# A second output-projection tile cut to seven rows a partition, its rest fetched in 8 KB pieces through GpSimd's queue

## The chip, the cores and the metric

One core of one Trainium2 chip runs the whole program. The metric is the device time of one execution in microseconds. The kernel before takes 393.38 us, the median of three runs (393.32 to 393.49).

## The reference

The program is one decode step of a transformer block with adaptive layer norm, for eight sequences of one token each, all in float32. The part that matters here is attention over a window of 2,048 cached positions and the projection by `wo` behind it:

```python
W = min(4096, max(256, Sk // 4))                      # 2048 of 8192 positions
q = (x @ wq).reshape(B, Sq, Hq, Dh).transpose(0, 2, 1, 3)
k = repeat(k_cache[:, :, Sk - W:, :], rep, axis=1)    # 8 kv heads, 4 query heads each
v = repeat(v_cache[:, :, Sk - W:, :], rep, axis=1)
p = softmax(einsum("bhqd,bhkd->bhqk", q, k) * Dh**-0.5)
o = einsum("bhqk,bhkd->bhqd", p, v)
A = o.transpose(0, 2, 1, 3).reshape(B, Sq, Hq * Dh) @ wo    # wo: 4096 x 512
...
mod = (silu(c) @ w_mod).reshape(B, 6, 1, 512)         # sa, ca, ga, sb, cb, gb
h = layernorm(x) * (1 + ca) + sa
x = x + ga * A(h)
h = layernorm(x) * (1 + cb) + sb
x = x + gb * (relu(h @ w1 + b1) ** 2 @ w2 + b2)
```

## The kernel before

Everything that the program needs from HBM is read once, about 165 MB, nearly all of it K and V.

**Loads and their order.** A list `loads` fixes the order: the two parts of `w_mod`, `wq`, then K and V tiles of 4 MB (32 KB in each of 128 partitions), with the `wo` tiles put between them, and the MLP's weights last. `pump` walks the list and stops at the first entry for whose size no buffer is free: there are four big buffers of 4 MB (in the tile `home`) and one small buffer of 2 MB (the tile `small`). `done(key)` gives a buffer back and calls `pump` again. All these loads are issued by SyncE (SP in the profile), one after the other on one queue, and SP waits in that order for the buffers to come free. The small buffer carries in turn the second part of `w_mod`, the `wo` tiles 0, `far`, 1, 2 and half of `w1`.

**A loop over 38 steps `s`.** Two steps belong to one K tile: VectorE transposes it (`transposes`, L216), TensorE makes the scores (`scores`, L387). A softmax follows every fourth step. Five steps later the V tile is multiplied (`weighted`, L473), and after every fourth of those steps `gather` (L508) sorts one kv head's output into `oT`, in which entry `i` of eight stands for the rows `8p + i` of a `wo` tile.

**The output projection.** `project_o(j)` multiplies `oT` with `wo` tile `j` (1,024 rows, 2 MB) and adds up in `wo_ps`. It runs at `s` = 14, 22, 30 and after the loop. Tile 0 is already held in another form: each group of 32 rows gives its first 28 rows to four partitions, seven rows each, so that the tile has 14 KB in each of 128 partitions. The last four rows of each group (128 rows in all, 256 KB) are the entry `far`. `far` is loaded in three pieces by SP (L143, L144) into a few partitions of the small buffer, which GpSimd (POOL) has cleared before (L139). Four small matmuls (L537) with the selector `fsel` bring the matching rows of `oT` into `oX`, and `far_rows` (L549, at `s` = 18) adds these rows' share. `gather` uses another split of its columns for the kv heads of tile 0.

**What frees what.** `project_o(1)` frees the small buffer at `s` = 22, and the next entry of the list, `wo` tile 2, is issued then by SP, behind the V load that stands ahead of it.

Of the kernel before, what the change touches and what calls it, by code (L numbers as in the profile page):

```python
# [19 lines left out]
def tile_adaln_cached_attention_mlp(  # L20
# [52 lines left out]
    eps = consts.tile([P, 1], F32, name="eps")  # L73
    nc.vector.memset(eps, EPS)
    fsel = consts.tile([P, 4, P], F32, name="fsel")
    nc.gpsimd.memset(fsel, 0.0)
    for y in range(2):
        nc.gpsimd.tensor_copy(
            fsel[:, :, 32 * y : 32 * y + 12].rearrange("p r (q a) -> p r q a", a=4),
            ident.rearrange("p (y a r q) -> p y r q a", y=2, a=4, r=4)[:, y, :, :3],  # L80
        )
    nc.gpsimd.tensor_copy(
        fsel[:, :, H : H + 32].rearrange("p r (h x) -> p r h x", x=4)[..., 3],
        ident.rearrange("p (h r q) -> p r h q", r=4, q=4)[..., 3],
    )
    oX = consts.tile([P, 8, 32], F32, name="oX")

# [15 lines left out]
    def load(key):  # L103
        kind, i = key
        held[key] = free[size_of(key)].pop(0)
        if key == ("wq", 0):
            return
        t = slots[size_of(key)][held[key]]
        if kind in "KV":

            hk, c = divmod(i, 2)
            v = k_cache[4 * c : 4 * c + 4, hk] if kind == "K" else v_cache[c::2, hk]
            v = v[:, SK - W :, :].rearrange("u (p j) d -> p u (j d)", j=NJ)
            cuts = (0, big // 2, big) if key == ("V", 2 * HKV - 1) else (0, big)
            for x, y in zip(cuts, cuts[1:]):
                nc.sync.dma_start(t[:, x:y], v[..., x:y])
            return

        def rows(o, v):
            n = v.shape[1] * v.shape[2]  # L120
            nc.sync.dma_start(t[:, o : o + n].rearrange("p (a n) -> p a n", n=v.shape[2]), v)

        w1v = w1.rearrange("(p kc) n -> p kc n", p=P)

        def wo_rows(j):

            r = 2 * REP * DH
            if j == 0:
                v = wo[:r].rearrange("(b s) n -> b s n", s=32)[:, :28].rearrange("b (g i) n -> b g (i n)", i=7)
                nc.sync.dma_start(t[:, : 7 * D], v)  # L130
                return
            v = wo[j * r : (j + 1) * r, :].rearrange("(p i) n -> p (i n)", p=P)
            nc.sync.dma_start(t[:, : big // 2], v)

        if kind == "wo":
            wo_rows(i)
        elif kind == "far":

            nc.gpsimd.memset(t[:H], 0.0)  # L139
            v = wo[: 2 * REP * DH].rearrange("(h q s) n -> q h s n", q=4, s=32)[:, :, 28:]  # L140
            v = v.rearrange("q h r n -> q h (r n)")
            for y in range(2):
                nc.sync.dma_start(t[32 * y : 32 * y + 12, : 4 * D], v[:3, 4 * y : 4 * y + 4])  # L143
            nc.sync.dma_start(t[3:32:4, 4 * D :], v[3])  # L144
        elif kind == "mod":

            v = w_mod.rearrange("(p kc) n -> p (kc n)", p=P)
            nc.sync.dma_start(t, v[:, big:] if i else v[:, :big])
        elif kind == "wq":

            o = base[held["wq", 0]]
            nc.sync.dma_start(home[:, o : o + 2 * big], wq.rearrange("(p k) n -> p (k n)", p=P))
        elif kind == "tail":
            wo_rows(HKV // 2 - 1)
# [12 lines left out]

    loads = [("mod", 0), ("mod", 1), ("wq", 0), ("wq", 1), ("K", 0), ("K", 1)]
    for n in range(2, 2 * HKV):
        if n == 9:  # L170
            loads.append(("far", 0))
        if n in (4, 11, 13):
            loads.append(("wo", (4, 11, 13).index(n)))
        loads += [("K", n), ("V", n - 2)]
    loads += [("V", 2 * HKV - 2), ("V", 2 * HKV - 1), ("tail", 0), ("w1", 0), ("w2", 0)]
    at = [0]
# [6 lines left out]
    def done(*keys):  # L183
        for k in keys:
            free[size_of(k)].append(held.pop(k))
        pump()
# [306 lines left out]
    def gather(hk):  # L493

        o = OS_.pop(hk)
        b = slice(H * (hk % 2), H * (hk % 2) + H)
        pp = ps_m.tile([P, 512], F32, name="m_ps", tag="m_ps")
        for x in range(2):
            to = pp[b].rearrange("p (d x e i) -> p x e d i", x=2, e=2, i=8)[:, x]
            cuts = [(to, o.rearrange("p e (d i) -> p e d i", i=8))]  # L500
            if hk < 2:
                o = o.rearrange("p e (q s) -> p (e q) s", s=32)
                cuts = [
                    (to[..., :7], o[:, :, :28].rearrange("p a (g i) -> p a g i", i=7)),
                    (to[..., 7].rearrange("p e (r q) -> p e q r", r=4), o[:, :, 28:]),
                ]
# [12 lines left out]

    def project_o(j):  # L520

        last = j == HKV // 2 - 1
        key = ("tail", 0) if last else ("wo", j)
        w = slot(key, D)
        for i in range(8 if j else 7):
            nc.tensor.matmul(
                wo_ps[32 * (i % 4) : 32 * (i % 4) + 32, :],
                oT[:, i, :],
                w[:, i, :],
                start=(j == 0 and i < 4),  # L530
                stop=(last and i >= 4),
            )
        if j == 0:

            px = ps_m.tile([P, 512], F32, name="m_ps", tag="m_ps")
            for r in range(4):
                nc.tensor.matmul(px[:, 32 * r : 32 * r + 32], fsel[:, r], oT[:, 7, :], start=True, stop=True)  # L537
            px = px[:, :P].rearrange("p (r b) -> p r b", b=32)
            nc.scalar.copy(oX[:H, :4], px[:H])
            nc.scalar.copy(oX[:32, 4:], px[H : H + 32])  # L540
        if not last:
            done(key)

    def far_rows():

        w = slot(("far", 0), D)
        for r in range(8):
            k = H if r < 4 else 32
            nc.tensor.matmul(  # L549
                wo_ps[32 * (r % 4) : 32 * (r % 4) + 32, :], oX[:k, r], w[:k, r, :], start=False, stop=False  # L550
            )
        done(("far", 0))

    def late_tiles():

# [13 lines left out]
    for s in range(N + PV_LAG + 1):  # L569
        g, i = divmod(s, C)  # L570
        q, h = divmod(s, 2)
        v = s - PV_LAG
        soft = 1 <= g <= HKV
        ends = v >= C and v % C == 0
        if i == 1 and soft and g < HKV:
            soft_e(g - 1)
        if s < N:
            transposes(q, 2 * h, 0)
        if 1 <= s <= N:
            scores((s - 1) // 2, 2 * ((s - 1) % 2) + 1)  # L580
            if i == 0:
                soft_a(g - 1)
        if s < N:
            transposes(q, 2 * h, 1)
        if i == 1 and soft:
            soft_f(g - 1)
        if v > C and v % (2 * C) == 1 and v < N:
            project_o(v // C // 2 - 1)
        if s == 18:
            far_rows()  # L590
        if 1 <= v <= N:
            weighted(v - 1, 1)
        if i == 0 and soft:
            soft_b(g - 1)
        if s < N:
            transposes(q, 2 * h + 1, 0)
        if i == 1 and soft:
            soft_g(g - 1)
            if g == HKV:
                rT, b1_in, b2_in, x1, h2T = late_tiles()  # L600
        if i == 0 and soft:
            soft_c(g - 1)
        if 1 <= v <= N and v % 2 == 0:
            parts(v // 2 - 1)
# [132 lines left out]
```

## Time and profile before

| What | Value |
|---|---|
| Median of three runs | 393.38 us (393.32 to 393.49) |
| The profiled execution: its own time | 393.28 us |
| The profiled execution: span from first to last instruction | 391.5 us |
| TensorE (PE), share of the span | 66% |
| VectorE (DVE), share of the span | 57% |
| ScalarE (ACT), share of the span | 12% |
| GpSimd (POOL), share of the span | 2% |
| SP's DMA queue, share of 16 engines | 98.3% |
| Read from HBM | 164.67 MB, 421 GB/s over the span |

The core has 16 DMA engines, and a transfer into 128 partitions is split over all of them. The profile gives their mean busy share, in 40 slices of the span or in any stretch that one asks for, and a share under 1 near the end says that some of them have run out of work. The rows of a stretch have the busy time of each compute engine, then the granted clock, the DMA share and the GB/s. In the list of waits a row names who waited, for whom, and then the total in us, the number of waits and the longest one.

### The profile page before, as it was taken

The page shows a single profiled execution, that of the slowest core. Times are in us where ns is not written, and L with a number is a line of the kernel's source. Part 1 is how long each engine was busy: PE and PEld are TensorE (multiplying, and loading weights), DVE is VectorE, ACT ScalarE, POOL GpSimd, SP SyncE. Part 2 cuts the span into 40 slices and gives each one's busy share as a digit, 9 for nine tenths or more (in the row PEclk, how much of TensorE's full clock was granted, in tenths as well). Part 3 has the DMA queues.
Part 4 walks back from the last instruction along what each step waited for, and adds up shares of the span by engine and source line. Part 5 has one row for each costly group of instructions (what it writes and reads, how often), then busy time and mean ns, then how long its engine had stood idle before and what let it go on. Part 6 is the DMA issues. An engine that isn't in the chain of part 4 may idle for free.

```text
span 391.5 us, 4765 instructions
## 1 busy us (share of the span) xinstructions
PE 258.8 (66%) x2050; PEld 79.7 (20%) x2050; DVE 224.0 (57%) x314; ACT 46.7 (12%) x91; POOL 5.9 (2%) x13
## 2 busy tenths in 40 slices
PE   0080959868437873797379828783773737996896
PEld 0030210112112320232122202220221212222333
DVE  1370099878057835874577456490776357854322
ACT  0120111311003100310031003100200003004010
POOL 1000000000000000030000000000000000000000
PEclk9996889998859996999599968988796969997999
DMA  8999999999999999999999999999999999999994
GB/s 330 437 429 426 437 435 442 435 424 411 431 432 432 437 432 435 430 427 429 444 417 435 430 432 432 427 429 427 415 445 437 429 429 431 425 423 424 421 432 190
DMA packets 6915, 165.04 MB, mean 422 GB/s; under 512 B 806, under 2 KB 974, under 8 KB 1230
## 3 DMA queue, kind: packets, MB, share of 16 engines
q1 hardware_dynamic: 6814, 164.70, 98.3%
q8 instruction: 16, 0.26, 0.3%
q10 hardware_dynamic: 80, 0.04, 0.0%
q14 instruction: 5, 0.04, 0.0%
HBM read 164.67 MB, written 0.07 MB: 421 GB/s over the span
## 4 chain that ended last, share of the span: by engine, by line
DMA 59%; DVE 22%; PE 14%; issue 4%; SPq 0%; ACT 0%; DVEq 0%; ACTq 0%
DMA home<-in_A_k_cache_dram 37%; DVE kT L216 12%; DMA home<-in_A_wq_dram 9%; DMA home<-in_B_w_dram 7%; DMA home<-in_A_v_cache_dram 6%; PE s_ps L387 5%; DVE pT L453 4%; PE p_ps L418 3%; PE m_ps L332 2%; PE o_ps L473 2%; DVE pr L446 2%; DVE mx L401 1%; DVE qbd L350 1%; PE m_ps L403 1%; PE m_ps L423 1%
## 5 line engine op out<-in xcount | busy, mean ns | idle before, releaser
L216 DVE STREAM_TRANSPOSE kT<-home 128x1024 f32<-128x1024 f32 x128 | 151.3, 1220 | 81.8 <-DMA home<-in_A_k_cache_dram 77.7
L387 PE MATMUL s_ps<-kT,qst 128*32 128x512 f32 x512 | 129.1, 1075 | 18.9 <-DVE kT L216 18.5
L473 PE MATMUL o_ps<-home,pT 128*32 128x256 f32 x1024 | 70.2, 397 | 11.1 <-DVE pT L453 10.5
L473 PEld LDWEIGHTS o_ps<-home,pT 128*32 128x32 f32 x1024 | 33.8, 118 | 103.1 <-issue 61.3
L403 PE MATMUL m_ps<-ident,mx 128*1 128x128 f32 x16 | 4.3, 364 | 58.3 <-DVE mx L401 58.3
L387 PEld LDWEIGHTS s_ps<-kT,qst 128*32 128x32 f32 x512 | 14.4, 115 | 38.2 <-DVE kT L216 30.1
L453 DVE STREAM_TRANSPOSE pT<-pr 128x2048 f32<-128x2048 f32 x8 | 18.2, 2275 | 1.0 <-ACT pr L436 1.0
L436 ACT ACTIVATE pr<-pr,own 128x512 f32<-128x512 f32 x16 | 17.8, 1223 | 0.3
L430 ACT ACTIVATE pr<-p_ps,nm 128x512 f32<-128x512 f32 x8 | 5.5, 687 | 96.2 <-DVE nm L427 96.2
L397 ACT COPY ss<-s_ps 128x512 f32<-128x512 f32 x8 | 4.7, 586 | 98.1 <-issue 69.2
L332 PE MATMUL m_ps<-home,oX 128*32 128x512 f32 x64 | 9.2, 741 | 10.1 <-DMA home<-in_A_wq_dram 10.1
L375 ACT COPY qst<-q_ps 32x128 f32<-32x128 f32 x32 | 8.2, 256 | 62.9 <-PE q_ps L364 62.6
L350 DVE COPY qbd<-m_ps 32x128 f32<-32x128 f32 x8 | 3.0, 373 | 18.8 <-PE m_ps L347 18.6
L403 PEld LDWEIGHTS m_ps<-ident,mx 128*1 128x1 f32 x16 | 0.7, 81 | 63.5 <-DVE mx L401 63.5
L250 PE MATMUL m_ps<-xsum,sel 128*128 128x1 f32 x2 | 0.6, 362 | 18.5 <-DVE xsum L248 18.5
L418 PE MATMUL p_ps<-ss,perm 128*128 128x512 f32 x16 | 11.8, 829 | 0.0
L427 DVE TENSOR_SCALAR nm<-m_ps 128x1 f32<-128x1 f32 x8 | 1.3, 158 | 16.4 <-PE m_ps L423 16.4
L508 PE MATMUL m_ps<-o_sb,pick 128*64 128x256 f32 (+2 forms) x40 | 9.7, 377 | 0.9 <-DVE o_sb L491 0.9
L446 DVE TENSOR_SCALAR pr<-pr,own 128x512 f32<-128x512 f32 x16 | 9.2, 657 | 0.8 <-ACT pr L430 0.8
L510 DVE STREAM_TRANSPOSE tr<-m_ps 64x512 f32<-64x512 f32 x8 | 5.7, 714 | 5.4 <-PE m_ps L508 5.2
L490 DVE TENSOR_SCALAR o_sb<-o_ps,bit 128x128 f32<-128x128 f32 x16 | 5.2, 327 | 5.5 <-PE o_ps L473 5.4
L228 DVE TENSOR_SCALAR e_sb<-e_sb 128x128 f32<-128x128 f32 x1 | 0.2, 227 | 12.9 <-ACT e_sb L227 12.9
(134 smaller groups left out, 131.7 us busy)
## 6 DMA issues: line engine op xcount, KB each, us to landing
home<-in_A_k_cache_dram SPq DMA_DIRECT2D x16, 4096.0 KB, 36.6
home<-in_A_v_cache_dram SPq DMA_DIRECT2D x15, 4096.0 KB, 22.4
home<-in_w_mod_dram SPq DMA_DIRECT2D x1, 4096.0 KB
small<-in_A_wo_dram SPq DMA_DIRECT2D x2, 2048.0 KB, 25.4
home<-in_A_v_cache_dram SPq DMA_DIRECT2D x2, 2048.0 KB, 21.5
small<-in_w_mod_dram SPq DMA_DIRECT2D x1, 2048.0 KB
home<-in_A_wo_dram SPq DMA_DIRECT2D x1, 2048.0 KB
home<-in_B_w_dram SPq DMA_DIRECT2D x1, 2048.0 KB
```

What stands on the lines that cost most here:

```text
L216: nc.vector.transpose(KTS[q, j][:, rows], k[:, rows, 32 * j : 32 * j + 32])
L332: nc.tensor.matmul(pqs[r][32 * g : 32 * g + 32, :], hT[:, kc, :], w[:, 4 * r + g, :], start=(kc == 0), stop=(kc == NQ - 1),)
L350: nc.vector.tensor_copy(qbd[b, 4 * r : 4 * r + 4, j].rearrange("p g (b t) -> p t g b", t=REP), pT_[b].rearrange("p (t g b) -> p t g b", t= ...
L375: nc.scalar.copy(own[b, :, :, i, 0], pq[b, :P].rearrange("p (c m t) -> p c m t", c=2, t=REP))
L387: nc.tensor.matmul(s_ps[0][32 * g : 32 * g + 32, :], qst[hk % 2][:, P * (4 * c + u) + 32 * j :][:, :32], kT[:, u], start=(c == 0 and j == ...
L403: nc.tensor.matmul(MX_[hk][0:1, :P], mx, ident, start=True, stop=True)
L418: nc.tensor.matmul(sp, perm, SS_.pop(hk), start=True, stop=True)
L436: nc.scalar.mul(X_[hk][..., w], pr, own[:, w : w + 1])
L446: nc.vector.tensor_scalar(X_[hk][..., w], pr, own[:, w : w + 1], None, op0=ALU.mult)
L453: nc.vector.transpose(PT_[hk].rearrange("p e j r -> p j e r"), X_.pop(hk).rearrange("p j x w -> p j (x w)"))
L473: nc.tensor.matmul(O_[n][32 * g : 32 * g + 32, : 2 * DH], PT_[hk][:, e, j : j + 2].rearrange("p j r -> p (j r)"), vt[:, j : j + 2, :].rear ...
L508: nc.tensor.matmul(dest, pick[:, x].rearrange("p t u -> p (t u)"), src, start=True, stop=True)
```

## The change

`wo` tile 1 gets the form of tile 0: seven rows to a partition, 14 KB in place of 16 KB. Its other 128 rows become a second `far` entry. They are loaded into the small buffer behind tile 1, not by SP but by GpSimd's queue, as 32 rows-of-four of 8 KB each: 12 of them into partitions 60 to 71, 12 more into the same partitions, and 8 into every fourth partition from 99. GpSimd clears all 128 partitions of the buffer first. Ahead of each of the three transfers stands a very small one that reads 7, 13 or 14 words of `b1` into a tile `step` which nothing reads. It moves on the place in the row of 16 DMA engines at which GpSimd's queue begins its next transfer, so that the pieces are to fall to engines 7 to 9 (eight pieces each) and once more to engines 8 to 15 (one each).

The selector `fsel` is written a second time by GpSimd for the new places, `project_o(1)` runs seven groups of matmuls in place of eight and four selector matmuls more, `far_rows(1)` runs at `s` = 25, and `wo` tile 2 goes behind the second `far`, one K and V tile later in the list.

```diff
-            if j == 0:
-                v = wo[:r].rearrange("(b s) n -> b s n", s=32)[:, :28]...
+            if j < 2:
+                v = wo[j * r : (j + 1) * r].rearrange("(b s) n -> b s n", s=32)[:, :28]...
                 nc.sync.dma_start(t[:, : 7 * D], v)
...
-            nc.gpsimd.memset(t[:H], 0.0)
-            v = wo[: 2 * REP * DH].rearrange("(h q s) n -> q h s n", q=4, s=32)[:, :, 28:]
+            r = 2 * REP * DH
+            v = wo[i * r : (i + 1) * r].rearrange("(h q s) n -> q h s n", q=4, s=32)[:, :, 28:]
             v = v.rearrange("q h r n -> q h (r n)")
-            for y in range(2):
-                nc.sync.dma_start(t[32 * y : 32 * y + 12, : 4 * D], v[:3, 4 * y : 4 * y + 4])
-            nc.sync.dma_start(t[3:32:4, 4 * D :], v[3])
+            nc.gpsimd.memset(t if i else t[:H], 0.0)
+            if i == 0:
+                for y in range(2):
+                    nc.sync.dma_start(t[32 * y : 32 * y + 12, : 4 * D], v[:3, 4 * y : 4 * y + 4])
+                nc.sync.dma_start(t[3:32:4, 4 * D :], v[3])
+            else:
+                ways = [(7, t[60:72, : 4 * D], v[:3, :4]), (13, t[60:72, 4 * D :], v[:3, 4:]), (14, t[99:P:4, : 4 * D], v[3])]
+                for j, (n, d, src) in enumerate(ways):
+                    nc.gpsimd.dma_start(step[:n, j : j + 1], b1[:n].rearrange("(a n) -> a n", n=1))
+                    nc.gpsimd.dma_start(d, src)
...
     for n in range(2, 2 * HKV):
-        if n == 9:
-            loads.append(("far", 0))
-        if n in (4, 11, 13):
-            loads.append(("wo", (4, 11, 13).index(n)))
+        if n in (9, 13):
+            loads.append(("far", n // 13))
+        if n in (4, 11, 14):
+            loads.append(("wo", (4, 11, 14).index(n)))
...
-            if hk < 2:
+            if hk < 4:
...
-        for i in range(8 if j else 7):
+        for i in range(8 if j > 1 else 7):
...
-        if j == 0:
+        if j < 2:
...
+            else:
+                nc.scalar.copy(oX[:, :4], px)
+                for b in (0, 32):
+                    nc.scalar.copy(oX[b + 32 : b + 64, 4:], px[b : b + 32])
...
-    def far_rows():
+    def far_rows(j):
...
-        done(("far", 0))
+        done(("far", j))
+        if j == 0:
+            far_columns((60, 28), 96)
+            nc.gpsimd.memset(oX[:, 4:], 0.0)
...
-        if s == 18:
-            far_rows()
+        if s in (18, 25):
+            far_rows(s // 25)
```

`far_columns(ys, rest)` is the old code that clears and fills `fsel`, now with the places as arguments. The changed kernel is 21 lines longer ahead of its end, so its line numbers are higher.

The first place is SP's queue around `wo` tile 2 (`small<-in_A_wo_dram 128x4096`), between the K and V loads of the list's places 12 to 15. Before:

```order
L116 DMA home<-in_A_k_cache_dram 128x1x8192 [waits DMAHW5_49,DVE_49]
L116 DMA home<-in_A_v_cache_dram 128x1x8192 [waits DMAHW6_49,PE_49]
L133 DMA small<-in_A_wo_dram 128x4096 [waits DMAHW7_49]
L116 DMA home<-in_A_k_cache_dram 128x1x8192 [waits DMAHW0_49,DVE_49]
L116 DMA home<-in_A_v_cache_dram 128x1x8192 [waits DMAHW1_49,PE_49]
L116 DMA home<-in_A_k_cache_dram 128x1x8192 [waits DMAHW2_49,DVE_49]
```

SP issued tile 2 ahead of a K and a V load. The same place of the same queue in the changed kernel:

```order
L122 DMA home<-in_A_k_cache_dram 128x1x8192 [waits DMAHW5_49,DVE_49]
L122 DMA home<-in_A_v_cache_dram 128x1x8192 [waits DMAHW6_49,PE_49]
L122 DMA home<-in_A_k_cache_dram 128x1x8192 [waits DMAHW0_49,DVE_49]
L122 DMA home<-in_A_v_cache_dram 128x1x8192 [waits DMAHW1_49,PE_49]
L139 DMA small<-in_A_wo_dram 128x4096 [waits DMASW5_49,DMASW3_49,DMAHW7_49,DMASW1_49,Pool_49]
L122 DMA home<-in_A_k_cache_dram 128x1x8192 [waits DMAHW2_49,DVE_49]
```

Tile 2 has moved behind one more K and V load, and SP waits there for GpSimd's three transfers (`DMASW`) too.

The second place is GpSimd's own program from the first clearing of `small` to its end. Before:

```order
L139 MEMSET small 64x4096 [waits DMAHW5_49,PE_49]
L560 MEMSET pr_1646 128x448 [waits DVE_49]
L732 UNCONDITIONAL_BRANCH
L732 ISA [waits barrier_Pool_Activation_PE_DVE_SP_gather]
```

GpSimd had one instruction for `far` and issued no transfer. In the changed kernel:

```order
L148 MEMSET small 64x4096 [waits DMAHW5_49,PE_49]
L81 MEMSET fsel 128x512 [waits PE_49,Pool_49]
L83 COPY fsel<-ident 128x4x12 [waits Pool_49]
L83 COPY fsel<-ident 128x4x12
L87 COPY fsel<-ident 128x4x8
L573 MEMSET oX 128x128 [waits DVE_49,PE_49,Activation_49]
L148 MEMSET small 128x4096 [waits DMAHW2_49,DMAHW1_49,DMAHW7_49,DMAHW0_49,PE_49]
L156 DMA step<-in_B_b_dram 7x1
L157 DMA small<-in_A_wo_dram 12x1x2048 [waits Pool_49]
L156 DMA step<-in_B_b_dram 13x1
L157 DMA small<-in_A_wo_dram 12x1x2048
L156 DMA step<-in_B_b_dram 14x1
```

The second clearing and six transfers have come to it (the sixth, of 8 pieces, follows the last row).

The third place is TensorE at step 25, where the scores (`s_ps`) of a new head begin. Before:

```order
L418 MATMUL p_ps<-ss,perm 128x512
L473 MATMUL o_ps<-home,pT 32x256 x8
L423 MATMUL m_ps<-ones,m_1252 128x1
L387 MATMUL s_ps<-kT,qst_111 32x512 x4
L473 MATMUL o_ps<-home,pT 32x256 x8
L459 MATMUL m_ps<-zs,tsel 64x8
```

The fourth row's scores were followed at once by a V product. In the changed kernel:

```order
L431 MATMUL p_ps<-ss,perm 128x512
L486 MATMUL o_ps<-home,pT 32x256 x8
L436 MATMUL m_ps<-ones,m_1275 128x1
L400 MATMUL s_ps<-kT,qst_112 32x512 x4
L567 MATMUL wo_ps<-small,oX 32x512 x8
L486 MATMUL o_ps<-home,pT 32x256 x8
L472 MATMUL m_ps<-zs,tsel 64x8
```

The eight matmuls of `far_rows(1)` have come in ahead of the V product.

More of the change, by code (lines that the diff above doesn't have):

```diff
@@ L75, in tile_adaln_cached_attention_mlp, with far_columns @@
     fsel = consts.tile([P, 4, P], F32, name="fsel")
-    nc.gpsimd.memset(fsel, 0.0)
-    for y in range(2):
+    oX = consts.tile([P, 8, 32], F32, name="oX")
+    step = consts.tile([16, 3], F32, name="step")
+    def far_columns(ys, rest):
+        nc.gpsimd.memset(fsel, 0.0)
+        for y, m in enumerate(ys):
+            nc.gpsimd.tensor_copy(
+                fsel[:, :, m : m + 12].rearrange("p r (q a) -> p r q a", a=4),
+                ident.rearrange("p (y a r q) -> p y r q a", y=2, a=4, r=4)[:, y, :, :3],
+            )
         nc.gpsimd.tensor_copy(
-            fsel[:, :, 32 * y : 32 * y + 12].rearrange("p r (q a) -> p r q a", a=4),
-            ident.rearrange("p (y a r q) -> p y r q a", y=2, a=4, r=4)[:, y, :, :3],
-        )
[L82 to L86, printed above, removed]
+            fsel[:, :, rest : rest + 32].rearrange("p r (h x) -> p r h x", x=4)[..., 3],
+            ident.rearrange("p (h r q) -> p r h q", r=4, q=4)[..., 3],
+        )
+    far_columns((0, 32), H)
     big = NJ * DH
@@ L127, in wo_rows @@
             r = 2 * REP * DH
-            if j == 0:
-                v = wo[:r].rearrange("(b s) n -> b s n", s=32)[:, :28].rearrange("b (g i) n -> b g (i n)", i=7)
+            if j < 2:
+                v = wo[j * r : (j + 1) * r].rearrange("(b s) n -> b s n", s=32)[:, :28].rearrange("b (g i) n -> b g (i n)", i=7)
                 nc.sync.dma_start(t[:, : 7 * D], v)
@@ L137, in load @@
         elif kind == "far":
-            nc.gpsimd.memset(t[:H], 0.0)
-            v = wo[: 2 * REP * DH].rearrange("(h q s) n -> q h s n", q=4, s=32)[:, :, 28:]
+            r = 2 * REP * DH
+            v = wo[i * r : (i + 1) * r].rearrange("(h q s) n -> q h s n", q=4, s=32)[:, :, 28:]
             v = v.rearrange("q h r n -> q h (r n)")
-            for y in range(2):
-                nc.sync.dma_start(t[32 * y : 32 * y + 12, : 4 * D], v[:3, 4 * y : 4 * y + 4])
-            nc.sync.dma_start(t[3:32:4, 4 * D :], v[3])
+            nc.gpsimd.memset(t if i else t[:H], 0.0)
[8 more added lines that the diff above has]
+                    nc.gpsimd.dma_start(d, src)
         elif kind == "mod":
@@ L538, in project_o @@
             px = px[:, :P].rearrange("p (r b) -> p r b", b=32)
-            nc.scalar.copy(oX[:H, :4], px[:H])
-            nc.scalar.copy(oX[:32, 4:], px[H : H + 32])
+            if j == 0:
+                nc.scalar.copy(oX[:H, :4], px[:H])
+                nc.scalar.copy(oX[:32, 4:], px[H : H + 32])
+            else:
+                nc.scalar.copy(oX[:, :4], px)
+                for b in (0, 32):
+                    nc.scalar.copy(oX[b + 32 : b + 64, 4:], px[b : b + 32])
         if not last:
             done(key)
-    def far_rows():
-        w = slot(("far", 0), D)
+    def far_rows(j):
+        w = slot(("far", j), D)
         for r in range(8):
-            k = H if r < 4 else 32
+            k = P if j else H if r < 4 else 32
             nc.tensor.matmul(
@@ L551, in far_rows @@
             )
-        done(("far", 0))
+        done(("far", j))
+        if j == 0:
+            far_columns((60, 28), 96)
+            nc.gpsimd.memset(oX[:, 4:], 0.0)
     def late_tiles():
```

## The prediction

> **What bounds the kernel now.** I read the page first, from its DMA line to the chain that ended last.
>
> ```profile
> span 391.5 us, 4765 instructions
> DMA  8999999999999999999999999999999999999994
> q1 hardware_dynamic: 6814, 164.70, 98.3%
> q8 instruction: 16, 0.26, 0.3%
> DMA 59%; DVE 22%; PE 14%; issue 4%; SPq 0%; ACT 0%; DVEq 0%; ACTq 0%
> ```
>
> The DMA engines are busy from the first slice to the last, and SP's queue (q1) alone fills 98.3% of them: 164.70 MB in 0.983 x 16 x 391.5 = 6,157 engine-us, or 26.75 GB/s for each engine. So 8 KB take 0.306 us on one engine, 16 KB 0.612 us and 32 KB 1.22 us. The bytes don't change. What can change is how they lie on the 16 engines, since the end is set by the engine that is done last. Next come the stretches at the end of the loads (the share and GB/s are the last columns):
>
> ```profile
> core 0: us, PE busy (x) PEld busy (x) DVE busy (x) ACT busy (x) POOL busy (x), PEclk, DMA share, GB/s
> 379.00:382.00 3.00, 3.00 (x33) 0.84 (x22) 0.20 (x1) 0.27 (x1) 0.00 (x0) 1.00 1.00 426
> ...
> 382.90:383.90 1.00, 1.00 (x4) 0.38 (x2) 0.78 (x3) 0.00 (x0) 0.00 (x0) 1.00 0.85 344
> 384.00:385.00 1.00, 1.00 (x25) 0.64 (x28) 0.00 (x0) 0.00 (x0) 0.00 (x0) 1.00 0.82 340
> 385.10:386.40 1.30, 1.21 (x46) 0.94 (x36) 0.00 (x0) 0.00 (x0) 0.00 (x0) 1.00 0.72 273
> 386.40:386.90 0.50, 0.23 (x8) 0.23 (x12) 0.00 (x0) 0.00 (x0) 0.00 (x0) 1.00 0.75 287
> 386.90:387.40 0.50, 0.50 (x28) 0.50 (x24) 0.00 (x0) 0.00 (x0) 0.00 (x0) 1.00 0.32 119
> 387.50:388.00 0.50, 0.50 (x24) 0.24 (x13) 0.00 (x0) 0.00 (x0) 0.00 (x0) 1.00 0.00 0
> ```
>
> The share goes from 1.00 to 0.82 = 13/16, then to 0.72 (between 11 and 12 sixteenths), and to nothing at 387.4. I read it so: three engines are done near 383.9 us, two more near 385.1, and eleven only at about 387.4. (0.72 lies between 11 and 12 sixteenths; I take eleven.) The imbalance is worth (3 x 3.5 + 2 x 2.3) / 16 = 0.9 us if it were shared out perfectly. That is the ceiling, 0.24% of the time. A change of this kernel under about 0.2% (0.79 us) can hardly be told from none.
>
> Does the end follow the last transfers? The chain's last pieces and three rows of the list of waits, each from its own late stretch:
>
> ```profile
> 360.97 25.66 DMA home<-in_B_w_dram
> 386.63 0.04 issue
> 386.67 1.76 PE m_ps L690 x48
> ```
>
> ```profile
> PE m_ps L690 <- DMA home<-in_B_w_dram: 0.4, 1, 0.4
> PE o_ps L473 <- DMA home<-in_A_v_cache_dram: 0.3, 1, 0.3
> DVE kT L216 <- DMA home<-in_A_k_cache_dram: 1.4, 1, 1.4
> ```
>
> It does, but barely. The last product waits 0.4 us for `w2`. A load of `w2` that is earlier by more brings more only if the compute chain ahead of it starts earlier too. That chain begins with the last K tile, for which DVE waits 1.4 us (stretch 325 to 352), and meets one more wait for V of 0.3 us. All these loads stand behind the change in the queue, so they come earlier by the same amount as the lagging engines.
>
> **What is taken from SP's queue.** `wo` tile 1 loses 256 KB, 16 KB on each engine: 0.61 us less for all 16. The same bytes come back as 32 pieces of 8 KB on GpSimd's queue. Where they go as the change says, engines 8 and 9 get nine pieces (2.75 us), 7 gets eight (2.45), 10 to 15 one (0.31), 0 to 6 none. Net: 0 to 6 minus 0.61 us, 10 to 15 minus 0.31, engine 7 plus 1.84, 8 and 9 plus 2.14.
>
> If 7, 8 and 9 are the three early engines, they end at 383.9 + 2.14 = 386.0 us, still ahead of the rest at 387.4 - 0.31 = 387.1. Each of nine pieces may then cost 0.12 us more, 0.43 us in all, before these engines set the end, and 0.46 us before the end is later than now. The gain is that of the slower of the other groups: 0.31 us if one of 10 to 15 is last today, 0.61 us if one of 0 to 6 is.
>
> **What a piece costs from a second queue.** No GpSimd transfer stands in the trace, so I bound it. The nearest thing is ScalarE's queue (q10), which loads `xc` into SBUF beside SP's; the list of queues from 5 to 14 us has
>
> ```profile
> q1 hardware_dynamic: 158, 3.85, 99.8%
> q10 hardware_dynamic: 64, 0.03, 1.2%
> ```
>
> 64 packets took 1.2% of 16 x 9 us = 1.7 engine-us, 0.027 us each, and SP's queue still filled 99.8%: a second queue into SBUF took its own bytes' time and left no hole that shows. On the other side stands the program's own instruction fetch (q8 above): 16 packets of 16 KB in 0.3% of 6,264 = 18.8 engine-us, or 1.17 us each against 0.61 at the rate of q1. By that row a piece costs 0.59 us. A gain below the byte time is excluded, since the bytes still have to move; so 0.31 to 0.59 us. I take 0.33, nearer to q10, because its data, too, go to SBUF, while q8's go elsewhere. The `step` words and the completion marks are some eight tiny packets an engine, 0 to 8 x 0.027 = 0.2 us; I take 0.1.
>
> The sum is minus 0.3 to minus 0.6, plus 0.1: about minus 0.4 us on the lagging engines, and by the waits above the end can follow.
>
> A rule speaks against this change: the Trainium skill, in "DMA: Bandwidth & Descriptors", section "Rules for kernel authors", says that spreading DMAs over SP, ACT and GpSimd does not help bandwidth, since all run on the same 16 engines. By it alone the sum would be 0 and the time 393.4; the share of 0.82 at 384 us shows that here the engines are not equally loaded, which that rule does not treat.
>
> **What is added beside the path.** These rows carry it: GpSimd's groups of instructions, TensorE's instructions of L537 and L549, the timeline from 249 us on, and three waits (the start's, DVE's between 246 and 320 us, and the chain's at 290).
>
> ```profile
> L139 POOL MEMSET small<- 64x4096 f32 x1 | 3.5, 3510 | 168.2 <-PE wo_ps L526 168.2
> L560 POOL MEMSET pr<- 128x448 f32 x1 | 0.5, 472 | 183.9 <-DVE pT L453 183.9
> ```
>
> ```profile
> L537 PE MATMUL m_ps<-oT,fsel x8: 276/276/297, 170.6 to 171.4; 128*128 128x32 f32 x8
> L549 PE MATMUL wo_ps<-small,oX x16: 587/600/613, 208.8 to 210.2; 64*32 64x512 f32 x8, 32*32 32x512 f32 x8
> ```
>
> ```profile
> 249.17 1.92 PE L526 MATMUL wo_ps<-small,oT 128*32 128x512 f32 x16
> 280.81 1.98 PE L387 MATMUL s_ps<-kT,qst 128*32 128x512 f32 x8
> 283.72 0.54 SPq L116 DMA_DIRECT2D home<-in_A_v_cache_dram  x1
> 289.98 0.53 SPq L116 DMA_DIRECT2D home<-in_A_k_cache_dram  x1
> ```
>
> ```profile
> ACT L227 <- DMA xc_in<-in_xc_dram: 13.9, 1, 13.9
> DVE kT L216 <- DMA home<-in_A_k_cache_dram: 29.8, 4, 9.2
> 289.98 26.80 DMA home<-in_A_k_cache_dram
> ```
>
> GpSimd waits 183.9 us between its old instructions, so rewriting `fsel` is free. The second clearing is as long per partition as the first: from 251.1 (the end of `project_o(1)`, 249.17 + 1.92) to 254.6 us. Then come six transfers. The pieces of engine 8 and six completion marks, 15 packets, take turns with SP's 32 KB packets; the four `xc` loads, eight packets an engine, needed 13.9 us that way, so 15 need some 26 us. They land near 281 us. `far_rows(1)` stands behind the scores that run from 280.81 to 282.8, so the margin is about 2 us and a late landing is possible. Queued behind it on PE are a V product, the denominator's matmul and the scores; DVE waits for these, and SP's V load at 283.72 and `wo` tile 2 behind it. But the next K tile is awaited for 26.8 us from 289.98 on, so several us of delay end inside that wait; beyond it the cost would be one for one.
>
> `wo` tile 2 is issued near 285 us in place of 262. It lands behind the K and V loads ahead of it, and `project_o(2)` needs it at about 335. SP is held up till 285, and its next load was issued at 289.98 anyway, so nothing is late. TensorE gets eight matmuls in `far_rows(1)` (L549's 16 records: 1.4 + 0.6 = 2.0 us), the four selector matmuls (0.8 + 0.3 = 1.1 us), and four more pieces in `gather`, less one group of `project_o`. DVE's four waits for K in that part, 29.8 us in all, cover them. Without that cover they would cost about 3 us.
>
> **The rivals.** *Slower, by the price of a piece.* If a piece costs 0.59 us as q8's row has it, engines 8 and 9 end at 383.9 - 0.61 + 9 x 0.59 = 388.6, 1.2 us after today's 387.4: 394.6. It decides from 0.46 us a piece. For it: a fetch beside SP's queue does take twice its bytes' time. Against it: q10. Chance 0.18.
>
> *Slower, by the place.* No view shows which engines are the three early ones. If one of 7, 8 and 9 is among the eleven, it ends 2.14 us later: 395.5. For it: 11 of 16 engines are late. Against: the three end together (the share holds at 0.82 for a whole us), which fits engines of one kind, side by side, more than a scatter. Chance 0.17.
>
> *The pieces don't fall as the change says.* Twelve partitions could be spread singly over twelve engines, and the eight over eight: then the engines 0 to 7 carry three pieces, 0.92 us, for the 0.61 taken. Three of these eight at least are among the late eleven, and the end moves by plus 0.3: 393.7. Chance 0.06. The Trainium skill, same page, section "Why a DMA increments its semaphore by 16 and not by 1", has both: a GpSimd transfer goes to k consecutive engines from a round-robin cursor, but for some direct copies on trn2 it takes 16 engines. No row here shows which holds.
>
> *Better than the sum.* Were the share-out perfect, with 0.9 us: 392.5. It would need the eleven to shed more than the 0.61 us that is taken from each; only if fetches happened to fall otherwise. Chance 0.09.
>
> **How the numbers follow.** The forecast has 0.50: minus 0.4 us. From the profiled execution's 393.28 that gives 392.9, and from the median, which is 0.1 higher, 393.0. Its own range, from minus 0.6 to plus 0.1, is 392.8 to 393.5. The whole range reaches down to 392.6 and up to 395.6, which takes in both slower rivals at their worked prices and leaves out about one in ten. Faster by over 0.2% is only the last rival, 0.09. Slower is the two priced rivals, 0.35. Within 0.2% lie the forecast and the spread pieces, 0.56.
>
> **What would show it.** Right: the DMA share between 384 and 385 us is near 1 and falls to nothing in one step before 387.2; GpSimd's queue appears with pieces of 8 KB at about 0.31 us; DVE's wait for the last K tile begins and ends a little earlier; `far_rows(1)` waits little. Wrong by the price: the pieces are longer, and at the end only two or three engines are busy (share near 0.15) after 387.4. Wrong by the place: the same low share, but with pieces of 0.31 us. If the share near 384 us is still 0.82 with the old end, the early engines were not hit at all.

## The result, and the profile after

The changed kernel takes **397.66 us** (median of five runs, 397.25 to 397.7) against 393.38 before: a ratio of 1.0105 (95% interval 1.0091 to 1.012). It is 4.3 us slower, where 393.0 was forecast, and it lies 2.1 us above the upper end of the range.

The page of the changed kernel, from the span to the queues:

```profile
span 395.9 us, 4851 instructions
...
DMA  8999999999999999999999999999999999999993
...
q1 hardware_dynamic: 6814, 164.43, 97.8%
...
q0 software_dynamic: 288, 0.26, 0.2%
```

GpSimd's queue (q0) has appeared with its 0.26 MB, 32 pieces among 288 packets, the rest tiny. The DMA engines look as busy as before. So the engines were not short of work, and yet the same bytes took 4.4 us of span more. The chain of waits says where. Of before:

```profile
247.20 25.85 DMA home<-in_A_k_cache_dram
273.14 2.37 DVE kT L216 x2
```

And of the changed kernel:

```profile
247.33 29.36 DMA home<-in_A_k_cache_dram
276.78 2.37 DVE kT L229 x2
...
293.65 27.68 DMA home<-in_A_k_cache_dram
321.43 2.37 DVE kT L229 x2
...
365.17 25.80 DMA home<-in_B_w_dram
391.01 1.30 PE m_ps L711 x40
```

Both chains enter the same wait for K at 247 us. The changed kernel leaves it 3.6 us later (276.78 against 273.14), leaves the next one about 4.5 us later (293.65 + 27.68 = 321.33, where before had 289.98 + 26.80 = 316.78), and starts its last product 4.3 us later (391.01 against 386.67). Most of the loss has been made between 247 and 277 us, while the pieces flow. The list of queues from 258 to 286 us, first of before and then of the changed kernel (packets, MB, share of 16 engines):

```profile
DMA packets 487, 12.03 MB, mean 430 GB/s; under 512 B 58, under 2 KB 58, under 8 KB 58
...
q1 hardware_dynamic: 486, 12.01, 99.9%
```

```profile
DMA packets 655, 10.73 MB, mean 383 GB/s; under 512 B 303, under 2 KB 303, under 8 KB 303
...
q1 hardware_dynamic: 366, 10.45, 97.4%
q0 software_dynamic: 288, 0.26, 3.3%
```

This is the reading on which the rest stands. In 28 us 1.30 MB less were moved, which is 3.0 us at 430 GB/s. The engines were not idle: q1 alone was busy for 0.974 x 16 x 28 = 436 engine-us. But it moved 10.45 / 436 = 23.9 GB/s on an engine, where before it moved 12.01 / 447.6 = 26.8. SP's own packets became some 12% longer on average while 0.26 MB came in on another queue. q0's packets themselves needed only 3.3% of 448 = 14.8 engine-us, 0.9 us on an engine.

An average could also come from a few slow engines among sixteen. The trace's records of single packets decide it. The 32 pieces come in three bursts (261.5 to 266.5, 269.6 to 275.3 and 279.2 to 281.0 us). All 38 packets of 32 KB that SP's queue began between 262 and 266 us took longer than the usual 1.22 us (1.30 to 2.00, mean 1.54), and so did all 41 begun between 270 and 274 (1.39 to 1.94). All 21 begun between 267 and 269 and all 26 between 276 and 278, with no piece under way, took 1.21 to 1.24. Since no packet took over 2.0 us, each of the 16 engines began at least one in those 4 us. So every engine is slowed while the pieces flow, and none between the bursts.

The stretches at the end, for the part that is not lost there:

```profile
core 0: us, PE busy (x) PEld busy (x) DVE busy (x) ACT busy (x) POOL busy (x), PEclk, DMA share, GB/s
...
388.00:389.00 1.00, 0.38 (x16) 0.41 (x20) 0.00 (x0) 0.00 (x0) 0.00 (x0) 1.00 0.74 297
389.00:390.00 1.00, 1.00 (x48) 1.00 (x40) 0.00 (x0) 0.00 (x0) 0.00 (x0) 1.00 0.60 223
390.00:391.00 1.00, 0.58 (x23) 0.31 (x12) 0.00 (x0) 0.00 (x0) 0.00 (x0) 1.00 0.30 115
391.00:392.00 1.00, 0.99 (x36) 0.99 (x40) 0.00 (x0) 0.00 (x0) 0.00 (x0) 1.00 0.11 43
```

Before, the share was 0.72 from 385.1 to 386.4 and fell to nothing at 387.4. Now it trails off over 3 us, from 0.60 to 0.30 and 0.11: the engines end further apart than before, not closer.

### The profile page after: what moved, and what is told of

Read it like the earlier page. It is cut to its first block, busy times and chain, and to the rows that moved or that the text cites. A ratio compares the mean times of both kernels' runs of the same rounds, so it can differ in the third digit from the quotient of the medians.

```text
span 395.9 us, 4851 instructions
## 1 busy us (share of the span) xinstructions
PE 261.2 (66%) x2080; PEld 81.6 (21%) x2080; DVE 224.1 (57%) x314; ACT 47.5 (12%) x94; POOL 14.0 (4%) x25
## 4 chain that ended last, share of the span: by engine, by line
DMA 59%; DVE 22%; PE 14%; issue 4%; SPq 0%; ACT 0%; DVEq 0%; ACTq 0%
DMA home<-in_A_k_cache_dram 38%; DVE kT L229 13%; DMA home<-in_A_wq_dram 9%; DMA home<-in_B_w_dram 7%; DMA home<-in_A_v_cache_dram 5%; PE s_ps L400 4%; DVE pT L466 4%; PE p_ps L431 3%; PE m_ps L345 2%; PE o_ps L486 2%; DVE pr L459 2%; DVE mx L414 1%; DVE qbd L363 1%; PE m_ps L416 1%; PE m_ps L436 1%
## 5 line engine op out<-in xcount | busy, mean ns | idle before, releaser
L486 PE MATMUL o_ps<-home,pT 128*32 128x256 f32 x1024 | 69.4, 394 | 11.7 <-DVE pT L466 9.8
L148 POOL MEMSET small<- 64x4096 f32 (+1 forms) x2 | 7.0, 3509 | 208.4 <-PE wo_ps L539 168.3
L521 PE MATMUL m_ps<-o_sb,pick 128*64 128x224 f32 (+2 forms) x48 | 9.9, 345 | 0.9 <-DVE o_sb L504 0.9
```

Of the source, the lines that this page charges most:

```text
L148: nc.gpsimd.memset(t if i else t[:H], 0.0)
L486: nc.tensor.matmul(O_[n][32 * g : 32 * g + 32, : 2 * DH], PT_[hk][:, e, j : j + 2].rearrange("p j r -> p (j r)"), vt[:, j : j + 2, :].rear ...
```

## The experiments

Theory 1 (called A in the later expectations): a piece that is written by another DMA engine than the one which writes its partition in the large loads holds up all 16 engines. Theory 2: GpSimd's queue as such stretches SP's packets. Theory 3: the step transfers do it. The first four runs cross queue with place. Where the places change, the clearing of the buffer and the selector `fsel` change with them; those lines are left out of the cuts.

**SP's queue, the change's places.** No GpSimd transfer and no steps:

```diff
-                    nc.gpsimd.dma_start(step[:n, j : j + 1], b1[:n].rearrange("(a n) -> a n", n=1))
-                    nc.gpsimd.dma_start(d, src)
+                    nc.sync.dma_start(d, src)
```

> The three piece transfers go by SP's queue to the same partitions (60 to 71 twice, 99 to 127), without the step transfers; all else as changed. Theory 1 (places): a piece that is written by an engine into partitions that are not that engine's usual ones holds up all engines; then SP's bytes fall to 320 to 390 GB/s while the pieces run and the time is about 397. Theory 2 (queue): it is GpSimd's queue that holds up SP's packets; then the rate stays at 425 to 430 GB/s and only the three engines that carry nine pieces end later, by 2.75 - 0.61 = 2.1 us if they are late ones: 395.0 to 395.6.

**The change without its steps.** Only the first of the two lines is taken out.

> The changed kernel without the three step transfers; the three piece transfers stay on GpSimd's queue, to the same partitions. Theories 1 and 2: the loss comes with the pieces, 397.2 to 397.8. Theory 3 (steps): the tiny transfers and their completion marks cost the time; then 395.5 or less. The pieces may fall to other engines than in the changed kernel, which moves the end by up to 1 us either way.

**GpSimd's queue with the steps, other places.** The pieces go to partitions 0 to 11, 12 to 23 and 3, 7, ... 31:

```diff
+ways = [(7, t[0:12, : 4 * D], v[:3, :4]), (13, t[12:24, : 4 * D], v[:3, 4:]), (14, t[3:32:4, 4 * D :], v[3])]
```

> The changed kernel with the pieces, still by GpSimd's queue and with the steps, put into partitions 0 to 11, 12 to 23 and every fourth from 3 to 31, as SP's first far transfers use them. Theory 1: no hold-up where the writing engine is the usual one of these partitions, at least for the first and third transfer; 425 GB/s in these, and 394 to 395.5 in all. Theory 2: SP's packets are as long as in the changed kernel, 397.2 to 397.8.

**SP's queue, the first `far`'s places** (0 to 11, 32 to 43 and 3, 7, ... 31):

```diff
+ways = [..., t[0:12, : 4 * D], ... t[32:44, : 4 * D], ... t[3:32:4, 4 * D :], ...]
-                    nc.gpsimd.dma_start(step[:n, j : j + 1], b1[:n].rearrange("(a n) -> a n", n=1))
-                    nc.gpsimd.dma_start(d, src)
+                    nc.sync.dma_start(d, src)
```

> The seven-row tile with all pieces by SP's queue at the partitions of the first far (0 to 11, 32 to 43, every fourth from 3 to 31), no steps, nothing on GpSimd's queue. All theories: no hold-up, three engines later by 2.1 us: 395.0 to 395.6. At 397 or more the seven-row form itself would be what costs.

| Pieces by | Places | us (interval of the runs) | Ratio to before |
|---|---|---|---|
| GpSimd, steps (the change) | 60-71 twice, 99, 103, ... | 397.66 (397.25 to 397.7) | 1.0105 [1.0091, 1.012] |
| GpSimd, no steps | the same | 397.26 (397.19 to 397.57) | 1.0103 [1.0088, 1.0118] |
| SP, no steps | the same | 399.50 (399.23 to 399.85) | 1.0159 [1.0144, 1.0174] |
| GpSimd, steps | 0-11, 12-23, 3, 7, ... | 394.56 (394.35 to 394.76) | 1.0032 [1.0019, 1.0046] |
| SP, no steps | 0-11, 32-43, 3, 7, ... | 395.82 (395.69 to 396.01) | 1.0064 [1.0047, 1.008] |

The places decide, not the queue: 3.1 us on GpSimd's queue (397.66 - 394.56) and 3.7 on SP's (399.50 - 395.82). Theory 2 falls, since the loss is as large with no GpSimd transfer at all. Theory 3 falls, since taking the steps out brought 0.4 us at most (the two sets of runs overlap). The size was not foreseen everywhere: SP's run at 399.50 lies 2.5 us above what theory 1 had been given. The same list of queues from 258 to 286 us, of the run without steps and then of GpSimd's queue with other places:

```profile
DMA packets 560, 10.80 MB, mean 386 GB/s; under 512 B 206, under 2 KB 206, under 8 KB 206
```

```profile
DMA packets 692, 12.04 MB, mean 430 GB/s; under 512 B 300, under 2 KB 300, under 8 KB 300
...
q1 hardware_dynamic: 407, 11.76, 97.8%
q0 software_dynamic: 284, 0.26, 2.7%
```

Without the steps the rate stays down at 386 GB/s. With other places (and their clearing and selector) it is 430, as before, and q1 moves 11.76 / (0.978 x 448) = 26.8 GB/s on an engine again. What remains of the loss in that run (394.56 against 393.33 of the kernel before on the same chip, 1.2 us) shows at its end, which trails off as the changed kernel's does:

```profile
386.00:387.00 1.00, 1.00 (x45) 1.00 (x41) 0.00 (x0) 0.00 (x0) 0.00 (x0) 1.00 0.59 219
387.00:388.00 1.00, 0.57 (x24) 0.30 (x19) 0.00 (x0) 0.00 (x0) 0.00 (x0) 1.00 0.32 123
388.00:389.00 1.00, 1.00 (x40) 0.98 (x40) 0.00 (x0) 0.00 (x0) 0.00 (x0) 1.00 0.13 49
```

On SP's queue the pieces flow later; the lists from 278 to 298 us, of the first `far`'s places and then of the change's:

```profile
DMA packets 316, 8.04 MB, mean 402 GB/s; under 512 B 46, under 2 KB 46, under 8 KB 46
```

```profile
DMA packets 256, 6.08 MB, mean 304 GB/s; under 512 B 46, under 2 KB 46, under 8 KB 46
```

**Any foreign place, or only some?** Two runs with SP's queue: 12 pieces to partitions 12 to 23 and 12 to 44 to 55 (the same half as the places of the run at 395.82, twelve partitions further up), or to 64 to 75 and 96 to 107 (the other half).

```diff
+ways = [..., t[12:24, : 4 * D], ... t[44:56, : 4 * D], ... t[3:32:4, 4 * D :], ...]    # the one
+ways = [..., t[64:76, : 4 * D], ... t[96:108, : 4 * D], ... t[3:32:4, 4 * D :], ...]   # the other
```

> SP's queue issues the pieces, without steps: 12 to partitions 12 to 23, 12 to 44 to 55, 8 to 3, 7, ... 31. On SP's queue the pieces of the first two fall to engines 0 to 2, as in the run that sent them to 0 to 11 and 32 to 43 (395.82), so now they lie in partitions of engines 3 to 5, but in the same half, 0 to 63. Theory A1 (any partition of another engine holds up all engines): packets of SP's beside the pieces are stretched as in the run with SP's queue and the change's places, for 24 of its 32 pieces: about 398.5. Theory A2 (only a crossing of the halves 0 to 63 and 64 to 127 holds up): 395.8, no stretch.

> SP's queue issues the pieces, without steps: 12 to partitions 64 to 75, 12 to 96 to 107, 8 to 3, 7, ... 31; the first two fall to engines 0 to 2 and lie in partitions of engines 8 to 10, in the upper half, whole transfers at a time. Theory A1 (any foreign partition) and A2 (only a crossing of the halves) both expect the stretch of SP's packets and about 398.5. Rival (the trouble is partitions 60 to 71 alone, which lie across the boundary of the halves): 395.8.

Measured: 398.90 (398.73 to 399.14; ratio 1.0141 [1.0127, 1.0155]) and 399.08 (398.93 to 399.25; 1.0145 [1.0129, 1.0161]). Both are 3.1 to 3.3 us above 395.82. The bytes from 278 to 298 us, of the same half and of the other half:

```profile
DMA packets 262, 6.28 MB, mean 314 GB/s; under 512 B 46, under 2 KB 46, under 8 KB 46
```

```profile
DMA packets 257, 6.11 MB, mean 306 GB/s; under 512 B 46, under 2 KB 46, under 8 KB 46
```

It is neither the crossing of the halves nor the partitions 60 to 71: two other sets of places cost nearly the same. On SP's queue only the first `far`'s own places were free of it.

**The start really moved.** If that is the cause, the change's own partitions must be harmless for the engines that own them. I expected that a step whose words are read in two levels (7 x 2, then 13 x 2) would move the start of GpSimd's next transfer:

```diff
-ways = [..., (14, t[99:P:4, : 4 * D], v[3])]
+ways = [..., (14, t[3:32:4, 4 * D :], v[3])]
-nc.gpsimd.dma_start(step[:n, j : j + 1], b1[:n].rearrange("(a n) -> a n", n=1))
+if j < 2:
+    nc.gpsimd.dma_start(step[: 2 * n, j : j + 1], b1[: 2 * n].rearrange("(b a n) -> a b n", b=2, n=1))
```

> The changed kernel, but the first two steps read their words in two levels (14 words as 7 x 2, 26 as 13 x 2), so that each should really move the place at which GpSimd's queue begins; the third step is gone and the third transfer (8 pieces) goes to partitions 3, 7, ... 31. The pieces of the first two transfers go to partitions 60 to 71 as in the change. Theory A (an engine that writes into partitions which the large loads give to another engine holds up all 16; the steps of the change did not move the start, these do): both transfers fall to engines 7 to 9, which own these partitions, no packet of SP's is stretched between 257 and 285 us, and the time is that of the byte count: 393.0 (392.8 to 393.3) if 7 to 9 are the early engines, about 395.3 if they are late ones. Rival (these partitions, 60 to 71, or their being written twice, are the trouble, whoever writes): still about 397.5. Rival (a two-level step does not move the start either): the pieces fall to engines 0 to 5 into partitions 60 to 71, and the time stays at 397.3 to 397.7.

Measured: 394.86 (394.76 to 394.95; ratio 1.0037 [1.0025, 1.005]). The list from 258 to 286 us and the end:

```profile
DMA packets 661, 12.08 MB, mean 431 GB/s; under 512 B 268, under 2 KB 268, under 8 KB 268
```

```profile
387.00:388.00 1.00, 0.79 (x31) 0.52 (x20) 0.00 (x0) 0.00 (x0) 0.00 (x0) 1.00 0.12 47
388.00:389.00 1.00, 0.80 (x30) 0.80 (x34) 0.00 (x0) 0.00 (x0) 0.00 (x0) 1.00 0.06 25
389.00:390.00 1.00, 0.92 (x28) 0.39 (x18) 0.01 (x1) 0.00 (x0) 0.00 (x0) 1.00 0.00 0
```

Twenty-four pieces go to the partitions of the change, twice over, by the same queue, and the hold-up is gone: 431 GB/s. So the partitions are not at fault, and the steps of the change did not do what they were for. (The last 8 pieces were moved too; a run below has them in the same place and the hold-up back.) But the time is not 393.0 either. After 388 us the share is 0.06 = 1/16: one engine works alone till 389.0, 1.6 us after the end of before. That is close to the picture which the prediction gave for a wrong choice of engines (two or three of them left).

**The same engines, places shifted by one engine's share** (56 to 67 in place of 60 to 71, nothing else):

```diff
-ways = [(7, t[60:72, : 4 * D], v[:3, :4]), (13, t[60:72, 4 * D :], v[:3, 4:]), ...]
+ways = [(7, t[56:68, : 4 * D], v[:3, :4]), (13, t[56:68, 4 * D :], v[:3, 4:]), ...]
```

> The run with the moved start (394.86), with one thing different: the 24 pieces of the first two transfers go to partitions 56 to 67 in place of 60 to 71, one engine's share lower. Queue, steps and engines 7 to 9 stay. Theory A (the engine of a piece must be the one to which the large loads give its partition): SP's packets are stretched again beside the pieces, and the time is about 397.5. Rival (it was the real step, or the engines 7 to 9 themselves, that made the difference): 394.9, no stretch.

Measured: 395.93 (395.67 to 396.13; ratio 1.0062 [1.0047, 1.0077]), 1.07 us above the run before it.

```profile
DMA packets 649, 11.55 MB, mean 413 GB/s; under 512 B 272, under 2 KB 272, under 8 KB 272
```

The hold-up is back, so the two-level step alone is not what helps. But it is smaller than I expected (397.5): 0.53 MB less than in the run with the places right, 1.2 us at 431 GB/s.

**Other engines, each in its own places**, to look for three early ones: 6 to 8 writing 56 to 67, 5 to 7 writing 52 to 63, and 3 to 5 writing 12 to 23 and 44 to 55. The last run sends engines 3 to 5 to 60 to 71. In each the first number sets the step:

```diff
+ways = [(6, t[56:68, : 4 * D], ...), (13, t[56:68, 4 * D :], ...), ...]
+ways = [(5, t[52:64, : 4 * D], ...), (13, t[52:64, 4 * D :], ...), ...]
+ways = [(3, t[12:24, : 4 * D], ...), (13, t[44:56, : 4 * D], ...), ...]
+ways = [(3, t[60:72, : 4 * D], ...), (13, t[60:72, 4 * D :], ...), ...]
```

> As the run with the shifted places, but the two steps bring the start to engine 6 (12 words as 6 x 2, then 13 x 2), so that engines 6 to 8 write partitions 56 to 67, which are theirs. Theory A: no stretch. In the run with engines 7 to 9 one of the three ended last, alone, at 389.0 us. If that was engine 9 and 6 is an early one, the end is set by the untouched engines, less 0.3 us: 393.0 (392.8 to 393.4). If engine 6 or 8 is a late one, 394.9 again.

> The same with the start at engine 5 (10 words as 5 x 2) and partitions 52 to 63, which belong to engines 5 to 7. Theory A: no stretch. 393.0 (392.8 to 393.4) if all three are early engines, about 394.9 if one of them is a late one. Of the three runs with engines 5 to 7, 6 to 8 and 7 to 9 those at 394.9 share a late engine.

> GpSimd's queue with real steps (6 words as 3 x 2, then 13 x 2) that bring the start to engine 3 for both transfers of 12 pieces, and places that belong to engines 3 to 5: partitions 12 to 23 and 44 to 55. The last 8 pieces go to partitions 3, 7, ... 31. No stretch of SP's packets by theory A. The runs with engines 5 to 7 and 6 to 8 (395.6) and 7 to 9 (394.9) ended with one to three of these engines alone, so 6, 7 or both are late engines. If 3, 4 and 5 are all early ones the time is 393.0 (392.8 to 393.3), a little under before; if one is a late one, 394.9 to 395.6.

> The run with the moved start (engines 7 to 9 writing partitions 60 to 71, 394.86), with the first step of 6 words in place of 14, so that engines 3 to 5 write partitions 60 to 71. It differs from the run just above only in the places. The run shifted by one engine was held up by some 1.2 us, less than the changed kernel's 3.1 for 32 pieces. Theory A, every wrong piece costs alike: 24/32 of 3.1, 2.3 us over the run with engines 3 to 5 in their own places. Rival, only the distance or the crossing of the halves makes it dear: still over 1.2 us, but nearer 3. Rival, a wrong piece at another place costs as little as the shift by one: 1.2 us.

| Engines meant | Places | us (lowest to highest) | Ratio to before |
|---|---|---|---|
| 6-8 | their own | 395.58 (394.21 to 395.7) | 1.0047 [1.0034, 1.0059] |
| 5-7 | their own | 395.61 (395.59 to 395.8) | 1.0056 [1.0043, 1.0068] |
| 3-5 | their own | 395.67 (395.55 to 395.89) | 1.0062 [1.005, 1.0075] |
| 3-5 | 60-71 | 398.05 (397.89 to 398.26) | 1.0122 [1.0108, 1.0135] |

The lists from 258 to 286 us of engines 3 to 5 in their own places and of the same engines at 60 to 71:

```profile
DMA packets 664, 12.04 MB, mean 430 GB/s; under 512 B 272, under 2 KB 272, under 8 KB 272
```

```profile
DMA packets 634, 11.09 MB, mean 396 GB/s; under 512 B 271, under 2 KB 271, under 8 KB 271
```

These two differ in the places alone (with their clearing and selector), and the wrong ones cost 2.38 us; 24/32 of the changed kernel's 3.1 had been expected, 2.3. The bytes agree: 0.95 MB less is 2.2 us. The sharpest pair is the last run and the one at 394.86. Their kernels differ in one number, the 6 or 14 words of the first step; places, clearing and selector are the same. The one takes 398.05 us at 396 GB/s, the other 394.86 at 431: the same partitions are harmful or harmless by the start of the queue alone.

With the places right none of the four sets of three engines helps: each median is 1.5 to 2.4 us above before, at a rate of 430 or 431 GB/s. Engines 5 to 7 and 6 to 8 came out 0.7 us above the 394.9 that was expected for a late engine among them (of the six runs of engines 6 to 8 one was at 394.21, the others at 395.43 to 395.7; why isn't known). The end of the run with engines 3 to 5:

```profile
387.00:388.00 1.00, 1.00 (x46) 1.00 (x41) 0.00 (x0) 0.00 (x0) 0.00 (x0) 1.00 0.32 109
388.00:389.00 1.00, 0.58 (x24) 0.32 (x18) 0.00 (x0) 0.00 (x0) 0.00 (x0) 1.00 0.11 41
389.00:390.00 1.00, 1.00 (x40) 0.83 (x32) 0.00 (x0) 0.00 (x0) 0.00 (x0) 1.00 0.07 25
```

One or two engines are left over after 388 us, again.

No run of these beats the kernel before. A split that gives pieces only to the engines that are early was not found: the profile's views name no engine, and only sets of three neighbours were tried.

## Why the prediction was wrong, point by point

- **What bounds the kernel: right.** The end followed the loads one for one. What was lost at 277 us was still lost at the end, as the chain shows.
- **Where the pieces go: this step failed first.** "Where they go as the change says, engines 8 and 9 get nine pieces" was taken over from the change. The run without steps has the same low rate and nearly the same time, and the run whose steps are read in two levels has full rate with 24 of the pieces in the same places. So the change's steps did not bring engines 7 to 9 to these partitions. The prediction had a rival of this kind with a chance of 0.06 (the pieces spread singly over engines 0 to 11), but priced it by byte counts alone at 393.7. The Trainium skill, "DMA: Bandwidth & Descriptors", section "Why a DMA increments its semaphore by 16 and not by 1", has the number of engines follow from the slowest dimension, with an exception on trn2 by which some direct copies use all 16. If steps of 7, 13 and 14 single words fall under that exception, they leave the start where it was, and the two-level form moves it; the runs at 397.26 and 394.86 agree, though no row here names an engine and the page doesn't say which copies it means.
- **What a piece costs: right for its own engine, and the larger term was missing.** I took 0.33 us and gave 0.31 to 0.59. In the run with other places q0 took 2.7% of 448 = 12.1 engine-us: 32 x 0.306 = 9.8 for the pieces, and 2.3 for the tiny packets, 0.14 us on an engine (0.1 taken). In the change it took 14.8, so a piece cost at most (14.8 - 2.3) / 32 = 0.39. But the price was not paid there. I read from q10 that a second queue "left no hole that shows" and priced a piece on its own engine alone. The change slowed SP's packets on all engines, by 10.45 MB at 23.9 in place of 26.8 GB/s: 436 - 390 = 46 engine-us, 2.9 us on each. This term the prediction put at nothing. No rival had a cost that one piece lays on 16 engines.
- **The place of the early engines: the forecast failed here too, and the rival held in kind.** With the hold-up gone, engines 7 to 9 end 1.5 us above before and the other sets 2.2 to 2.4, where the rival said 2.1 (395.5). In the run with GpSimd's queue, the steps and other places it is 1.2 us (394.56 - 393.33, before's median on that chip). The two together are the result: 3.1 for the places and 1.2 for the unequal load (the tiny packets with it) make 4.3.
- **Beside the path: right.** These are rows of the changed kernel's timeline, in order of time: the clearing, the last piece's issue, the scores, `far_rows(1)`, and `wo` tile 2:

```profile
251.40 3.51 POOL L148 MEMSET small<- 128x4096 f32 x1 [40.15 <-DMA home<-in_A_k_cache_dram]
...
257.63 0.52 POOL L157 DMA_DIRECT2D small<-in_A_wo_dram  x1
...
284.45 1.99 PE L400 MATMUL s_ps<-kT,qst 128*32 128x512 f32 x8
...
286.24 1.92 PE L567 MATMUL wo_ps<-small,oX 128*32 128x512 f32 x16
...
289.80 0.45 SPq L139 DMA_DIRECT2D small<-in_A_wo_dram  x1
```

And the row of the last 8 pieces in the list of DMA issues (its last number is the time from issue to landing):

```profile
small<-in_A_wo_dram POOLq DMA_DIRECT2D x1, 64.0 KB, 25.2
```

The last piece was there at 257.63 + 25.2 = 282.8; I had said near 281. `far_rows(1)` ran right behind the scores at 286.24, for 1.92 us (2.0 said), and waited for nothing. The clearing took 3.51 us, as said, and `wo` tile 2 was issued at 289.80 (285 said); the chain has no wait for it.
- **The range** ended at 395.6 because the two slower rivals were priced singly. Even added up (1.2 and 2.1) they give 396.7; the hold-up was in neither.

## What to carry to other kernels

Before a byte count over DMA engines is turned into microseconds, ask which engine will write which partition: pieces fetched by other engines than those that write these partitions in the streaming loads can slow the whole stream, on GpSimd's queue and on SP's alike, and it does so while every engine reads as busy. A busy share of 1.00 doesn't show it; the bytes of q1 per busy engine-us do (23.9 against 26.8 here). And where a change relies on where a queue will start, run it once without the trick: if time and rate stay, the trick very likely does nothing.

## What the runs showed of the hardware that I had not expected

- **Pieces in foreign places slow all 16 engines.** While they flow, SP's 32 KB packets take 1.54 us on average in place of 1.22. 0.26 MB in 32 pieces cost 3.1 us by GpSimd's queue and 3.7 by SP's. With 24 pieces it was 2.4 us (engines 3 to 5 at 60 to 71), 3.1 and 3.3 (SP, the two runs above), and only 1.1 when the places are shifted by one engine's share. Why the last is cheaper stays open, and so does whether the last 8 pieces of the undisturbed runs lay in their engines' own places: the rate shows only that they did no harm.
- That engine and partition belong together is in the Trainium skill, "DMA: Bandwidth & Descriptors", section "The descriptor swizzle": in a load of 128 partitions engine 7 writes 28 to 31 and 60 to 63, engine 8 writes 64 to 67 and 96 to 99, and so on. The places chosen by this rule ran at 430 to 431 GB/s in four runs, and those with 24 or 32 pieces elsewhere on GpSimd's queue at 383 to 413, so the runs agree; places 0 to 23 ran at 430, which fits if the single-level steps left the start at engine 0. The same page of the Trainium skill, section "Back-pressure in remote DMA", says, for copies between cores, that a saturated destination port holds up the engines that share the path. The loss here has that look within one core's loads, but no row shows a port, so this is argued and not shown.
- **A two-level step moves the start of GpSimd's queue.** The runs at 394.86 and 398.05 differ in its word count alone, and the rate is 431 or 396 GB/s. **A single-level one does not**, as far as the rates tell it: 383 GB/s with it, 386 without.
